# One-token decoder layer on one core: five engine programs with and without a block around them

## Chip, cores and metric

The kernel runs on one core of one Trainium2 chip. Its time is device microseconds of one execution, as the median of three runs. A core has five engines that run programs of their own and meet only through semaphores: TensorE (PE, with its weight loads as PEld), VectorE (DVE), ScalarE (ACT), GpSimd (POOL) and SyncE (SP). SP computes nothing here; it issues nearly all transfers.

## What is computed

Four sequences of one token each go through a pre-norm attention over the last 4096 positions of a key and value cache, and then through a gated network. All tensors are bfloat16.

```python
B, Sq, D = 4, 1, 576;  Hq, Hkv, Sk, Dh = 32, 16, 16384, 128;  F = 4608
W = min(4096, max(256, Sk // 4))
q = (x @ wq).reshape(B, Sq, Hq, Dh).transpose(0, 2, 1, 3)
k = jnp.repeat(k_cache[:, :, Sk - W:, :], rep, axis=1)
v = jnp.repeat(v_cache[:, :, Sk - W:, :], rep, axis=1)
scores = jnp.einsum("bhqd,bhkd->bhqk", q, k) * (Dh ** -0.5)
o = jnp.einsum("bhqk,bhkd->bhqd", softmax(scores), v)
attention = o.transpose(0, 2, 1, 3).reshape(B, Sq, Hq * Dh) @ wo
...
gate = einsum("bsd,df->bsf", x, W_gate);  up = einsum("bsd,df->bsf", x, W_up)
mlp = einsum("bsf,fd->bsd", gate * (gate > 0) * up, W_down)
...
h  = x + attention(layernorm(x))
h2 = h + mlp(layernorm(h))
```

## The kernel before

The window of keys and of values is 67 MB each, and the weights are some 25 MB more, so about 160 MB come in for little arithmetic. The cache is cut into 32 "duos": two key heads of one sequence, 2 MB of keys and 2 MB of values each. Four duos make a batch, so there are 8 batches.

A large tile, `pool`, holds four slots for keys and four for values. The query weights lie in the value slots at first, and the weights of the output projection and of the network take the same room after the attention. `prog_sync` goes through a list of transfers in a fixed order (lines 219 to 256); each waits until the last reader of its place is done. Query weights come first, then keys five duos ahead of the values, then the weights.

`prog_pool` makes constants: it clears tiles (L277 to L279, L283 to L287), builds an identity with an affine select (L280, and a second one at L288), and later finds, for each batch, the largest score over all partitions (L295). `prog_dve` waits for the identity before it builds its selectors (L376) and goes on to the first layer norm; the query projection on PE follows from that. For each half duo of keys DVE transposes the keys (L416), PE multiplies them with the queries (a helper, so nearly all of PE stands at L520), and at the end of a batch DVE takes the maximum (L419), ACT the exponentials (L344), DVE transposes the result (L435) and PE multiplies it with the values. After the last batch come the output projection, the second layer norm, the network's two wide matmuls and the down projection, whose weights come in nine pieces (L256). ACT and DVE write one half of the result each (L363, L513), SP stores it (L270) and waits until the store has landed (`S.wait("sync", "STORED")`).

All five programs are written with a small class, `Sched`. A first pass only counts: it gives every named operation the semaphore value at which it will be done. A second pass emits the instructions, with waits on those values. `S.op` and `S.dma` address the engines through `S.engines`, that is `nc.sync`, `nc.scalar` and so on. In the second pass each program is called by the method of a block for its engine (last lines of the function).

Two places of the code appear in the profile where no operation of the kernel stands. L693 is the line that makes the builder, `_bacc.Bacc(...)`; four constants and a meeting of the five engines come from it. L116 is `with ExitStack() as es:`; what is emitted when the context managers close, the block among them, has this line.

Of the kernel before, what the change touches and what calls it, by code (L numbers as in the profile page):

```python
# [102 lines left out]
def bass_sequential_preLN__sliding_block_cached__glu_gated_reglu__decode_kernel(  # L103
# [12 lines left out]
    with ExitStack() as es:  # L116
# [75 lines left out]
        S = Sched()  # L192
# [479 lines left out]
        progs = [("gpsimd", prog_pool), ("sync", prog_sync), ("scalar", prog_act), ("vector", prog_dve), ("tensor", prog_pe)]  # L672
# [1 line left out]
        for _, p in progs:  # L674
            p(S)
        S.begin(True, nc, es)
        block = es.enter_context(nc.Block())
        for name, p in progs:
            getattr(block, name)(lambda e, p=p: p(S))


# [26 lines left out]
```

## Time and profile before

| | |
|---|---|
| median of 3 runs (lowest to highest) | 383.69 us (383.65 to 383.76) |
| profiled execution: from its first to its last instruction | 382.2 us, 3916 instructions |
| read from memory in it | 159.58 MB, 418 GB/s over the span |
| PE busy | 287.7 us (75%), mean granted clock 0.905 |
| DVE busy | 206.5 us (54%) |
| ACT busy | 53.5 us (14%) |
| POOL busy | 8.2 us (2%) |

The span runs from the first recorded instruction, at 0, to the end of the last one; the records resolve nanoseconds (the last ends at 382.199 us). The time of a run is taken outside the profile and is 1.49 us longer than this span; the trace has no record of those 1.49 us. Waiting is not counted as busy. Engine names with a q (SPq, POOLq) are the engine's sequencer, which runs semaphore, branch, drain and transfer-issuing instructions.

### The profile page before, as it was taken

How to read it: one execution, taken by the hardware profiler on the slowest of the kernel's cores; microseconds unless marked ns; L12 is line 12 of the kernel's file. 1: busy time of each engine (PE TensorE's matmuls, PEld its weight loads, DVE VectorE, ACT ScalarE, POOL GpSimd, SP SyncE). 2: the span in 40 equal slices, each digit the busy share in tenths (PEclk: the TensorE clock that was granted, in tenths of full speed). 3: DMA queues.
4: the chain of work that ended last, by engine and by line, in shares of the span. 5: the costliest groups of instructions: out<-in, count | busy, mean ns of one | idle time of the engine just before them, and what ended most of it. 6: DMA issues, size and time to landing. Idle time of an engine off the chain costs nothing.

```text
span 382.2 us, 3916 instructions
## 1 busy us (share of the span) xinstructions
PE 287.7 (75%) x1697; PEld 124.5 (33%) x1712; DVE 206.5 (54%) x193; ACT 53.5 (14%) x129; POOL 8.2 (2%) x22
## 2 busy tenths in 40 slices
PE   0069749977997799669967996799589796956565
PEld 0053213322432243224322432243224233344331
DVE  0369789369437854774477548744865442042030
ACT  4021050021102110211021103010300021010020
POOL 4100000000000000000000000000000000000000
PEclk9999988997998799989998999899989996965677
DMA  8999999999999999999999999999999999999994
GB/s 307 434 424 422 436 422 429 431 425 427 426 429 430 424 429 430 425 429 429 429 425 430 425 427 432 424 430 427 427 430 425 427 431 424 419 430 424 420 416 198
DMA packets 12417, 159.84 MB, mean 418 GB/s; under 512 B 1384, under 2 KB 1520, under 8 KB 2672
## 3 DMA queue, kind: packets, MB, share of 16 engines
q1 hardware_dynamic: 12392, 159.59, 98.7%
q8 instruction: 13, 0.21, 0.2%
q14 instruction: 4, 0.03, 0.0%
q10 hardware_dynamic: 8, 0.00, 0.0%
HBM read 159.58 MB, written 0.00 MB: 418 GB/s over the span
## 4 chain that ended last, share of the span: by engine, by line
PE 50%; DVE 18%; issue 16%; ACT 6%; DMA 5%; SPq 3%; POOL 1%; POOLq 0%
PE sc L520 27%; PE pb L520 23%; DVE kT L416 6%; ACT P L344 5%; DMA pool<-in_B_W_down_dram 5%; DVE probT L435 4%; DVE rmx L419 4%; SPq L256 3%; POOL bcm L295 1%; DVE P L477 1%; DVE bias L431 0%; DVE rowsum L440 0%; DVE pmax L422 0%; DVE t L427 0%; DVE bmin L429 0%
## 5 line engine op out<-in xcount | busy, mean ns | idle before, releaser
L416 DVE STREAM_TRANSPOSE kT<-pool 128x2048 f32<-128x2048 f32 x64 | 144.5, 2291 | 54.4 <-DMA pool<-in_A_k_cache_dram 47.6
L520 PE MATMUL sc<-kT,qz 128*128 128x512 bf16 x497 | 133.1, 422 | 48.4 <-DVE kT L416 45.1
L520 PE MATMUL pb<-pool,prob 128*16 128x512 bf16 x512 | 118.5, 391 | 0.0
L520 PEld LDWEIGHTS sc<-kT,qz 128*128 128x128 bf16 x512 | 49.2, 102 | 128.6 <-DVE kT L416 53.2
L520 PEld LDWEIGHTS pb<-pool,prob 128*16 128x16 bf16 x512 | 44.0, 92 | 72.4 <-issue 19.0
L344 ACT ACTIVATE P<-sc,bias 128x512 f32<-128x512 f32 x32 | 22.2, 718 | 176.8 <-DVE bias L431 176.8
L419 DVE TENSOR_REDUCE rmx<-sc 128x2 f32<-128x2048 f32 x8 | 18.3, 2292 | 34.9 <-PE sc L520 34.9
L435 DVE STREAM_TRANSPOSE probT<-P 128x2048 f32<-128x2048 f32 x8 | 18.5, 2312 | 7.9 <-ACT P L344 7.9
L527 PE MATMUL pb<-ident_b,xn_bf 4*128 4x4 bf16 (+1 forms) x5 | 0.4, 175 | 19.6 <-ACT xn_bf L308 19.6
L329 ACT COPY cp<-pb 128x512 f32<-128x512 f32 x8 | 4.7, 585 | 67.9 <-PE pb L520 67.9
L520 PE MATMUL pb<-selT,cp 128*128 128x16 f32 x64 | 8.7, 269 | 4.4 <-ACT cp L329 4.4
L520 PEld LDWEIGHTS pb<-selT,cp 128*128 128x128 f32 x64 | 9.0, 208 | 6.5 <-ACT cp L329 5.4
L351 ACT CAST prob<-probT 128x1024 bf16<-128x1024 f32 x8 | 8.4, 1044 | 19.0 <-DVE rs L438 19.0
L444 DVE RECIPROCAL rs_sb<-pb 128x32 f32<-128x32 f32 x4 | 1.4, 339 | 17.8 <-PE pb L520 17.8
L507 DVE TENSOR_TENSOR P<-pb,P 128x288 bf16<-128x288 f32 (+1 forms) x2 | 0.8, 400 | 17.3 <-PE sc L520 17.3
L520 PE MATMUL pb<-pool,probT 128*4 128x288 bf16 x72 | 6.1, 310 | 5.4 <-DMA pool<-in_B_W_down_dram 5.4
L295 POOL PARTITION_ALL_REDUCE bcm<-pmax x8 | 3.1, 388 | 291.5 <-DVE pmax L422 291.5
L322 ACT COPY qz<-qrep 32x64 bf16<-32x64 bf16 x32 | 7.8, 244 | 7.3 <-DVE qrep L453 7.0
L520 PE MATMUL sc<-oX,pool 128*128 128x4 bf16 (+1 forms) x160 | 5.9, 172 | 3.7 <-DVE oX L480 3.7
L520 PE MATMUL pb<-pool,hnT 128*32 128x288 bf16 (+1 forms) x48 | 4.0, 405 | 6.0 <-DMA pool<-in_B_W_up_dram 6.0
L520 PE MATMUL sc<-pool,hnT 128*32 128x288 bf16 (+2 forms) x112 | 6.8, 366 | 0.6 <-DMA pool<-in_B_W_gate_dram 0.6
L520 PEld LDWEIGHTS sc<-oX,pool 128*128 128x128 bf16 (+1 forms) x160 | 5.8, 114 | 4.0 <-issue 3.9
(107 smaller groups left out, 80.1 us busy)
## 6 DMA issues: line engine op xcount, KB each, us to landing
pool<-in_A_k_cache_dram SPq DMA_DIRECT2D x32, 2048.0 KB, 27.9
pool<-in_A_v_cache_dram SPq DMA_DIRECT2D x32, 2048.0 KB, 25.9
pool<-in_A_wo_dram SPq DMA_DIRECT2D x4, 1152.0 KB, 21.7
pool<-in_B_W_gate_dram SPq DMA_DIRECT2D x2, 2304.0 KB, 24.8
pool<-in_B_W_up_dram SPq DMA_DIRECT2D x2, 2304.0 KB, 27.3
pool<-in_A_wq_dram SPq DMA_DIRECT2D x2, 2048.0 KB, 10.1
pool<-in_B_W_down_dram SPq DMA_DIRECT2D x2, 1296.0 KB, 24.1
pool<-in_B_W_down_dram SPq DMA_DIRECT2D x5, 432.0 KB, 25.8
```

The costliest lines, as they stand in the source:

```text
L256: lambda e, g0=g0, g1=g1, j0=j0, nj=nj: e.dma_start(out=wd_sb[:, g0:g1, j0 * D:(j0 + nj) * D], in_=B_W_down[g0 * 128 * JJ:g1 * 128 * JJ, : ...
L295: S.op(g, lambda e, n=n: e.partition_all_reduce(bcm[:, n % 2, :], pmax[:, n % 2, :], 128, bass_isa.ReduceOp.max), deps=deps, name=("PAR", n))
L322: S.op(a, lambda e, src=src, dst=dst: e.copy(out=dst, in_=src), deps=deps, name=("QZ", n) if g == 3 else None, signal=g == 3)
L329: S.op(a, lambda e: e.copy(out=cp[:, n % 2, :], in_=pb[PVB + n % 2]), deps=deps, name=("CP", n))
L344: S.op(a, lambda e, n=n, th=th, u=u: e.activation(out=P[:, th * 1024 + u:(th + 1) * 1024:2], in_=sc[:, th * 1024 + u:(th + 1) * 1024:2], f ...
L351: S.op(a, lambda e, n=n: e.copy(out=prob[:, n % 2, :, :, :], in_=probT[:, :, 0:NHB].rearrange("p t (r x) -> p r t x", x=4)), deps=deps, na ...
L416: S.op(v, lambda e: e.transpose(out=dst, in_=src), deps=deps, name=("TR", i))
L419: S.op(v, lambda e: e.tensor_reduce(out=rmx[:, n % 2, :], in_=sc[:, :].rearrange("p (x u) -> p u x", u=2), axis=AX.X, op=ALU.max), deps=[( ...
L435: S.op(v, lambda e: e.transpose(out=probT[:, :, :].rearrange("p t j -> p (t j)"), in_=P[:, :]), deps=[("EXP", n, 1)] + ([("CMP", n - 1)] i ...
L444: S.op(v, lambda e: e.reciprocal(out=rs_sb[:, b, :], in_=pb[OB][:, 64 + b * H:64 + (b + 1) * H]), deps=[("SUM", b)], name=("RS", b))
L477: S.op(v, lambda e: e.tensor_reduce(out=oS.rearrange("p (x b) -> p x b", b=B), in_=oM.rearrange("p (x s b) -> p x b s", s=8, b=B), axis=AX ...
L520: S.op(t, lambda e: e.matmul(o, lhsT=l, rhs=r, start=start, stop=stop, skip_group_check=skip), deps=deps, name=name, signal=name is not None)
```

## The change

The block is taken away. In the emitting pass the five programs are called one after the other, straight in the function, in the same order as before and as in the counting pass. The programs themselves, their waits, their transfers and the semaphores are the same text; the builder's line moves up by one (L693 becomes L692).

```diff
         S.begin(True, nc, es)
-        block = es.enter_context(nc.Block())
-        for name, p in progs:
-            getattr(block, name)(lambda e, p=p: p(S))
+        for _, p in progs:
+            p(S)
```

## Prediction

> **What bounds the kernel now.** I read the page's transfers and speeds first, then a table by stage, then the records of the two lines that are not the kernel's own work (L693 and L116), and last the start.
>
> ```profile
> DMA  8999999999999999999999999999999999999994
> q1 hardware_dynamic: 12392, 159.59, 98.7%
> ```
>
> The first line is the busy share of the 16 DMA engines in 40 slices, the second SP's and the other hardware queues' packets, MB and share. Only the first and the last slice have room. The table by stage (stretch, its length, then busy time of PE, PEld, DVE, ACT and POOL with counts, granted clock, DMA share, GB/s) says the same in more detail:
>
> ```profile
> 2.00:20.00 18.00, 0.43 (x8) 0.40 (x9) 3.83 (x20) 4.47 (x8) 3.61 (x8) 1.00 0.97 402
> 20.00:100.00 80.00, 63.71 (x372) 26.44 (x377) 60.70 (x47) 13.37 (x36) 0.78 (x2) 0.91 1.01 427
> ...
> 300.00:347.00 47.00, 36.03 (x306) 19.05 (x304) 15.21 (x16) 6.25 (x12) 0.39 (x1) 0.82 1.01 426
> 347.00:370.00 23.00, 12.17 (x223) 7.77 (x223) 3.86 (x18) 2.37 (x6) 0.00 (x0) 0.62 1.00 419
> 370.00:378.00 8.00, 4.44 (x60) 2.12 (x60) 1.93 (x6) 0.00 (x0) 0.00 (x0) 1.00 0.88 355
> 378.00:382.20 4.20, 1.60 (x12) 0.41 (x12) 0.45 (x1) 0.39 (x1) 0.00 (x0) 0.51 0.07 24
> ```
>
> From 2 to some 376 us the transfers set the pace, at 419 to 428 GB/s. What PE, DVE or ACT do earlier or later in between changes nothing, as long as SP's queue does not run dry. Only two places are outside this cover: what lies ahead of SP's first transfer (0 to 0.72 us), and what follows the last weights (378.3 to 382.2 us). The end is this chain (start, length, operation):
>
> ```profile
> 378.33 1.60 PE L520 MATMUL pb<-pool,probT 128*4 128x288 bf16 x12 [0.52 <-DMA pool<-in_B_W_down_dram]
> ...
> 379.98 0.45 DVE L513 CAST out_sb<-pb 4x288 bf16<-4x288 f32 x1 [7.98 <-PE pb L520]
> 380.50 0.35 SPq L270 DMA_DIRECT2D out_dram<-out_sb  x1
> ```
>
> PE ends, ACT and DVE write the halves side by side, SP stores. Behind that only the records of L116 are left (count, duration in ns, first and last start in us):
>
> ```profile
> L116 POOLq EVENT_SEMAPHORE  x2: 17/17/17, 382.0 to 382.1; - x2
> L116 POOLq DRAIN  x1: 502/502/502, 310.3 to 310.3; - x1
> L116 PEldq DRAIN  x1: 585/585/585, 379.4 to 379.4; - x1
> ...
> L116 SPq COMPARE_BRANCH  x1: 32/32/32, 381.8 to 381.8; - x1
> L116 SPq DRAIN  x1: 13/13/13, 382.0 to 382.0; - x1
> L116 SPq EVENT_SEMAPHORE  x1: 17/17/17, 382.1 to 382.1; - x1
> ```
>
> This is the block's end: each engine drains, POOL collects the five signals and releases all. SP comes last, because its branch carries the wait for the store.
>
> **The change part by part.** *The end.* The block's 12 instructions go: five drains, six semaphore instructions, SP's branch. In nanoseconds the records put SP's branch at 381.809, its drain at 381.978, POOL's two semaphore instructions at 382.015 and 382.093, the four releases at 382.136 to 382.148 (PE's lasts 51 ns, to 382.199, the end of the span). Four of the drains lie beside the store or long before it (PE 379.404, ACT 379.985, DVE 379.994, POOL 310.3) and set nothing; SP's path does: 0.032 for the branch, 0.137 from it to the drain, 0.221 from there to the end, 0.390 us together. What stays is the wait for the store. It needs another carrier; SP's semaphore instructions take 17 ns each in these records. Sum of the end: 0.390 − 0.017 = 0.373 us, and the last record ends at 381.809 + 0.017 = 381.826. Bounds of the carrier: 0.017 and the branch's 0.032, so 0.358 to 0.373; I take 0.37.
>
> *The entry.* The block is also entered, and a branch could hide there. SP's release in the builder's meeting (L693) ends at 0.658 and its first transfer issues at 0.721, 63 ns later. POOL's two semaphore instructions at the end stand 61 ns apart (382.032 to 382.093) with nothing in between. So at most 0.002 us is to be had at the entry on SP, and the trace has no branch there. Bounds: 0 and 0.002; I take 0. A loss at the entry isn't excluded and is the slower rival below.
>
> *The five programs.* The instructions, waits and transfers are the same, in the same order on each engine, so 0. Moving the code by a few instructions can move the moment at which instruction pages are fetched (13 packets of the first instruction queue, 4 of the second, 0.2% of the DMA engines' time). All of it lies under the transfers; 0.2% of 382 us is 0.8 us, and a page more would be one packet of 13, or 0.06 us.
>
> *Outside the span.* The runs' median exceeds the span by 383.69 − 382.20 = 1.49 us. No record shows what is in it. If some of it is work at the end that begins when an engine leaves the block, PE, ACT, DVE and POOL could do it earlier: they are done by 379.99, 380.40, 380.48 and 310.8, SP not before 381.83. So between 0 and 1.49 us more could go. The nearest row for what engines do when they leave a meeting is the start: released at 0.60 to 0.65, POOL and ACT issue their first own instruction at 0.717, so nothing but issue follows. I take 0 and keep 1.49 for the range.
>
> The Trainium skill, "Runtime: NRT & Kernel Launch", in "The ~15µs preamble/postamble breakdown", has the runtime add a barrier of its own behind the kernel, about 1.5 us, that waits for all engines, and only then the resets. By it the last engine to arrive still decides, the early ones gain nothing, and the sum remains the 0.37 by which SP arrives sooner; no record of this trace shows that barrier.
>
> **Sum:** the span goes from 382.20 to 381.83; on the median, with the same 1.49 us around it, 383.69 − 0.37 = 383.32 us, 0.10% less. About 0.2% (0.77 us) is what a measurement of this kernel can tell from no change, so this counts as the same.
>
> **The rivals.** *1. The meeting stays (no gain).* The change may not do what it says: something else, the builder's end or the launch, may put an equal meeting behind programs that end without a block. For it: the builder puts one at the start unasked (L693, same drains and semaphores). Against it: the records at the end all have the line of the context managers, none the builder's. Time 383.69.
>
> *2. The end shrinks by more (faster).* Four engines leave 1.3 us or more before SP, and their share of the 1.49 us outside the span goes under SP's wait. For it: 1.49 us is large beside a meeting of 0.37. Against: this time may as well lie ahead of the first record, and SP still has its own share. All of it gives 383.32 − 1.49 = 381.83, half of it 382.57; over 0.40 us of the 1.49 is needed to pass 0.2%.
>
> *3. The start chain gets later (slower).* The chain of waits begins on POOL:
>
> ```profile
> 0.89 3.52 POOL L279 MEMSET qz<- 128x4096 bf16 x1
> 14.82 0.28 POOL L280 TENSOR_SCALAR_AFFINE_SELECT ident_b<-ident_b 128x128 bf16<-128x128 bf16 x1 [10.41 <-issue]
> ```
>
> For 10.4 us POOL does nothing the profile shows between L279 and the affine select; the raw records have two instructions there that change POOL's configuration, and two more at L295. DVE, then ACT, then PE wait for it, until DVE has transposed the first duo and SP may load the fifth one at 28.82. If programs without a block were laid out so that this stall comes twice, or on a cold page, the chain is later by x. The cover: query weights and four duos are queued from the start, 4.5 + 4 × 2 MB (13.11 MB in decimal); by 28.0 us 385 GB/s × 28.0 us = 10.78 MB have landed, the other 2.33 MB last 5.4 us at 429 GB/s, to 33.4. From 28.82, less the 1.04 us from SP's first issue (0.721) to its first packet (1.76), that is 3.5 us. A start later by under 3.5 us costs nothing, beyond it one for one: a second stall of 10.35 us costs 6.8 us, 383.32 + 6.8 = 390.1. For it: the stall is there and nothing in the trace says what sets its length. Against it: POOL's program keeps its order, and the block's entry shows no branch on POOL (release at 0.598 to 0.615, first own instruction at 0.717). That the stall shrinks would bring nothing, since the transfers run full meanwhile (0.97 to 1.01).
>
> **How the numbers follow.** Forecast (0.37 us less) 0.44; rival 1 (no gain) 0.25; rival 2 (faster by more) 0.20; rival 3 (slower) 0.11. So faster 0.20, same 0.44 + 0.25 = 0.69, slower 0.11. The likeliest gives 383.32. For the range I leave out rival 3 whole (0.11) and the third of rival 2 in which over 1 us of the 1.49 goes (0.07): from 383.32 − 1.0 = 382.3 up to rival 1's 383.69 and, for what the moved pages may cost under full queues (at most the 0.5 us that lie between 383.69 and 384.2, two thirds of all that the instruction pages take now), 384.2.
>
> **What would show it.** Right: 3905 instructions (12 fewer, one new carrier of SP's wait), no records on L116 that drain or signal, SP's wait for the store as the last record near 381.83, first transfer still at 0.72, POOL's affine select still near 14.8, GB/s at 419 to 428 in the same stages. Rival 1: drains and semaphores behind the store under another line, span at 382.2. Rival 2: span 381.8 and a median less than 1.1 us above it. Rival 3: the affine select after 18.3 us, and a slice around 33 us with a DMA share clearly below 1.0. The forecast is wrong if the span falls by under 0.2 or over 0.6 us, or if any stretch between 2 and 376 us loses its full transfers.

## The result and the profile after

| | before | after |
|---|---|---|
| median (lowest to highest), 17 runs each | 383.76 us (383.50 to 384.16) | 382.96 us (382.70 to 383.26) |
| ratio, 95% interval | | 0.9977 (0.9970 to 0.9984) |
| span of the profiled execution | 382.2 us | 381.7 us |

The kernel is 0.80 us faster; by the interval, 0.61 to 1.15 us (383.76 × 0.0016 and × 0.0030). The middle of it is just beyond the 0.2% (0.77 us) that the prediction named as the least difference it could tell; the interval reaches to both sides of that.

The page of the kernel after, first the span, then the share of the DMA engines in 40 slices and the main queues:

```profile
span 381.7 us, 3920 instructions
...
DMA  8999999999999999999999999999999999999995
...
q1 hardware_dynamic: 12392, 159.59, 98.8%
```

3920 instructions are recorded, against 3916. The 12 of the block are gone and SP's new wait is there; but 1712 matmuls are recorded against 1697 before. Without these 15, which the trace of before lacks, there would be 3905, the number expected.

The table by stage of the kernel after (busy time of PE, PEld, DVE, ACT and POOL with counts, granted clock, DMA share, GB/s):

```profile
2.00:20.00 18.00, 0.35 (x6) 0.32 (x7) 3.83 (x20) 4.48 (x8) 3.60 (x8) 1.00 0.99 411
20.00:100.00 80.00, 64.22 (x371) 25.95 (x371) 59.82 (x46) 13.36 (x36) 0.78 (x2) 0.85 1.01 426
300.00:347.00 47.00, 36.94 (x305) 19.18 (x303) 15.21 (x16) 6.25 (x12) 0.39 (x1) 0.83 1.01 426
347.00:370.00 23.00, 12.92 (x226) 8.32 (x225) 3.58 (x17) 2.37 (x6) 0.00 (x0) 0.60 1.00 422
370.00:378.00 8.00, 6.07 (x60) 3.16 (x60) 2.21 (x7) 0.00 (x0) 0.00 (x0) 0.64 0.88 354
```

The transfers run as before: no stage differs by more than 9 GB/s. The start and the end, in the timeline of the kernel after (start, length):

```profile
0.72 0.88 SPq L230 DMA_DIRECT2D pool<-in_A_wq_dram  x2
...
14.89 0.28 POOL L280 TENSOR_SCALAR_AFFINE_SELECT ident_b<-ident_b 128x128 bf16<-128x128 bf16 x1 [10.49 <-issue]
...
379.86 0.45 DVE L513 CAST out_sb<-pb 4x288 bf16<-4x288 f32 x1 [7.54 <-PE pb L520]
380.38 0.35 SPq L270 DMA_DIRECT2D out_dram<-out_sb  x1
```

The first transfer goes out at 0.72 as before and the affine select comes at 14.89 instead of 14.82. What follows the store is one record, the second of SP's explicit waits in the last two microseconds (count, ns, first and last start):

```profile
L75 SPq EVENT_SEMAPHORE  x2: 17/17/17, 380.3 to 381.7; - x2
```

It begins at 381.683 and ends the span at 381.700. From the store's issue (380.379) this is 1.32 us; before it was 382.199 − 380.503 = 1.70 us. The difference is 0.38 us, and it is the meeting of the five engines with SP's branch ahead of it. So the span accounts for about half of the 0.80 us.

### The profile page after: what moved, and what is told of

Its sections match the earlier page's. It is cut to its first block, busy times and chain, and to the rows that moved or that the text cites. A ratio compares the mean times of both kernels' runs of the same rounds, so it can differ in the third digit from the quotient of the medians.

```text
span 381.7 us, 3920 instructions
## 1 busy us (share of the span) xinstructions
PE 293.9 (77%) x1712; PEld 125.8 (33%) x1712; DVE 206.8 (54%) x193; ACT 53.4 (14%) x129; POOL 8.2 (2%) x22
## 4 chain that ended last, share of the span: by engine, by line
PE 43%; DMA 23%; DVE 19%; ACT 6%; issue 5%; SPq 3%; POOL 1%; POOLq 0%
PE sc L520 22%; PE pb L520 21%; DMA pool<-in_A_k_cache_dram 18%; DVE kT L416 8%; DMA pool<-in_B_W_down_dram 5%; ACT P L344 4%; DVE probT L435 4%; DVE rmx L419 4%; SPq L256 3%; POOL bcm L295 1%; DVE P L477 1%; DVE bias L431 0%; DVE P L473 0%; DVE rowsum L440 0%; DVE t L427 0%
## 5 line engine op out<-in xcount | busy, mean ns | idle before, releaser
L520 PE MATMUL sc<-kT,qz 128*128 128x512 bf16 x512 | 138.5, 425 | 44.8 <-DVE kT L416 43.0
L520 PE MATMUL pb<-pool,probT 128*4 128x288 bf16 x72 | 7.8, 386 | 3.0 <-DMA pool<-in_B_W_down_dram 2.9
```

What stands on the lines that cost most here:

```text
L520: S.op(t, lambda e: e.matmul(o, lhsT=l, rhs=r, start=start, stop=stop, skip_group_check=skip), deps=deps, name=name, signal=name is not None)
```

## The experiments

One quantity carries them: the **part outside**, the time of a run less the span of the same run, as a mean over the runs. Spans are listed to 0.1 us. The part outside scatters by 0.03 us from run to run, so its mean over 10 runs or more is good to about 0.01 us. The spans scatter by some 0.2 us, and their means are good to 0.05 or 0.1 us only. In the 17 runs of the kernel after it is 1.30 us.

**1. The kernel before once more**, unchanged, to have its spans run by run.

> The kernel before, unchanged, so that its spans are listed run by run. Every theory: ratio to itself 1.000, median 383.7 to 383.8. What it tells apart is the part of a run outside the span (time less span), which is 1.3 us in the changed kernel. Theory A (the whole gain lies inside the span: the meeting's 0.37 us and some 0.4 us that the transfers or the entry gave): outside part 1.3, span 382.4. Theory B (engines that leave early also shorten what lies outside): outside part 1.5, span 382.2 to 382.3.

Measured: median 383.79 us, ratio 0.9998 (0.9990 to 1.0007), mean span 382.02, part outside 1.79; 33 more runs of the kernel before on the same chip give 382.04 and 1.79, and two other chips 1.79 and 1.80. So two things shrink: the span by 0.39 (382.04 to 381.65) and the part outside by 0.49 (1.79 to 1.30). That favours theory B, though its 1.5 was too low.

**2. The meeting alone put back**, without a block.

```diff
         for _, p in progs:
             p(S)
+        nc.all_engine_barrier()
```

> No block, but the builder's meeting of all engines (drains and semaphores) called behind the five programs. If all of the 0.80 us comes from the meeting at the end: back to 383.7, ratio 1.000 to before, span some 0.37 us above the changed kernel's 381.7. If part of it comes from the block's branches and the place of the code: it keeps that part, 0.2 to 0.4 us below before, ratio 0.9990 to 0.9995.

Measured: median 383.70 us, ratio 0.9999 (0.9990 to 1.0007), mean span 381.96, part outside 1.81. The call's records (L679):

```profile
L679 POOLq EVENT_SEMAPHORE  x2: 17/17/17, 381.8 to 381.9; - x2
L679 SPq DRAIN  x1: 7/7/7, 381.8 to 381.8; - x1
L679 SPq EVENT_SEMAPHORE  x1: 17/17/17, 382.0 to 382.0; - x1
...
L679 PEldq EVENT_SEMAPHORE  x1: 51/51/51, 382.0 to 382.0; - x1
```

The same signals as at the block's end, and the whole gain is gone: both the span and the part outside are back. The block's branches and the place of the code gave nothing that the runs can tell; but the interval reaches down to 0.9990, so a gain of up to 0.38 us from them is not excluded by the times alone. In the records SP's way from its wait (381.744) to the end (382.016) is 0.27 us, 0.12 less than with the block's branch; on the time that is below the interval.

**3. No meeting, but all five engines wait for the store.**

```diff
+        for e in ("gpsimd", "scalar", "vector", "tensor"):
+            S.wait(e, "STORED")
```

> No block and no meeting, but POOL, ACT, DVE and PE each wait on the store's semaphore as SP does, so all five leave together. Theory A (only the meeting's own 0.37 us in the span counts): as the changed kernel, ratio 0.9977 to 0.998, outside part 1.3. Theory B (leaving early counts): span as the changed kernel's, outside part back to 1.5, time 383.15 to 383.2, ratio 0.9983 to 0.9985.

Measured: median 383.46 us (383.27 to 384.97), ratio 0.9995 (0.9986 to 1.0003), part outside 1.79. The records of the waits:

```profile
L75 SPq EVENT_SEMAPHORE  x2: 17/17/17, 380.3 to 381.7; - x2
L75 ACTq EVENT_SEMAPHORE  x1: 17/17/17, 381.7 to 381.7; - x1
L75 POOLq EVENT_SEMAPHORE  x1: 17/17/17, 381.7 to 381.7; - x1
L75 DVEq EVENT_SEMAPHORE  x1: 21/21/21, 381.7 to 381.7; - x1
L75 PEldq EVENT_SEMAPHORE  x1: 51/51/51, 381.7 to 381.7; - x1
```

There is no drain and no signal between engines here, and the profiled execution ends at 381.756 against 381.700. Yet the part outside is back at 1.79. So it isn't the meeting that costs those 0.49 us but that the other engines leave late. Theory A falls; theory B is right about the mechanism. The median is still 0.3 us above what theory B gave, because theory B put the part outside at 1.5.

**4. Two meetings**, a second one behind the block of the kernel before.

```diff
-        block = es.enter_context(nc.Block())
-        for name, p in progs:
-            getattr(block, name)(lambda e, p=p: p(S))
+        with nc.Block() as block:
+            for name, p in progs:
+                getattr(block, name)(lambda e, p=p: p(S))
+        nc.all_engine_barrier()
```

> The kernel before with a second meeting of all engines behind the block. The second has no late engine to wait for, so it costs its own chain alone. If the meeting's price is its chain of signals: 0.25 to 0.4 us more than before, 384.0 to 384.15, ratio 1.0007 to 1.001, all of it in the span. If a meeting costs twice that, as the 0.80 us suggest: 384.5, ratio 1.002.

Measured: median 384.10 us (383.88 to 386.69), ratio 1.0013 (1.0000 to 1.0026), part outside 1.77. In the trace the first meeting ends at 381.932, the second at 382.264, 0.33 us later. The median rises by 0.31; the interval begins at 1.0000, for one of the 11 runs is far off (386.69), and the other ten lie between 383.88 and 384.32. So by the trace and the median a meeting with no late engine costs its own chain of signals, all of it in the span; a second one adds nothing outside. The other half of the 0.80 us is paid once, at leaving.

**5 to 8. Which engine is the last.** SP no longer waits for the store; one other engine does. POOL is shown:

```diff
-            S.wait("sync", "STORED")
...
         for _, p in progs:
             p(S)
+        S.wait("gpsimd", "STORED")
```

> No block; the wait for the store stands on POOL instead of SP, so SP leaves at 380.7 us and POOL is the last engine. Theory C (what lies outside the span is work of each engine in a fixed order, and the place of the late engine in that order decides): the part outside differs from the 1.30 us that SP last gave, between 1.1 and 1.8. Theory D (only that the engines don't arrive together matters): 1.30 us whichever engine is last, 382.95 us.

> The same with ACT as the only engine that waits for the store. Theory C: outside part other than 1.30 us by at least 0.05 for some of the four engines. Theory D: 1.30 us, 382.95 us.

> The same with DVE. Theory C: outside part other than 1.30 us, by its place in the order. Theory D: 1.30 us, 382.95 us.

> The same with PE, whose semaphore instruction takes 51 ns instead of 17, so the span is some 0.04 us longer. Theory C: outside part other than 1.30 us, by its place in the order. Theory D: 1.30 us, 382.99 us.

| last engine | median us | ratio (interval) | mean span | part outside |
|---|---|---|---|---|
| SP (the kernel after) | 382.96 | 0.9977 (0.9970 to 0.9984) | 381.65 | 1.30 |
| DVE | 383.05 | 0.9980 (0.9971 to 0.9989) | 381.59 | 1.42 |
| ACT | 382.92 | 0.9982 (0.9973 to 0.9992) | 381.60 | 1.46 |
| PE | 383.37 | 0.9989 (0.9980 to 0.9999) | 381.75 | 1.58 |
| POOL | 383.52 | 0.9996 (0.9987 to 1.0006) | 381.70 | 1.87 |

The waits with POOL last:

```profile
L75 SPq EVENT_SEMAPHORE  x1: 17/17/17, 380.7 to 380.7; - x1
L75 POOLq EVENT_SEMAPHORE  x1: 17/17/17, 382.1 to 382.1; - x1
```

The spans agree within 0.16 us, but the part outside runs from 1.30 to 1.87. Theory D falls. What lies behind the last instruction depends on the engine: with POOL last nearly the whole gain is gone, though there is no meeting and four engines have left. This suggests a simpler form of theory C: each engine has a tail of its own, and the latest end of a tail ends the run. The lengths in the last column serve as tails in the sums below; each also holds whatever of a run lies ahead of its first record, which is the same for all engines. So only their differences are shown, and only these count in the sums.

**9 to 11. Several late engines, and POOL almost late.** These test that form. In 9, POOL waits for the store beside SP; in 10, ACT, DVE and PE do; in 11, POOL waits only until DVE has written its half of the result.

```diff
+        S.wait("gpsimd", "STORED")
```

```diff
+        for e in ("scalar", "vector", "tensor"):
+            S.wait(e, "STORED")
```

```diff
+        S.wait("gpsimd", "OUT1")
```

> No block, SP and POOL both wait for the store, the other three leave early. Theory C' (each engine has a tail of its own behind its last instruction, the latest end counts: 1.87 us for POOL, 1.30 for SP): span 381.65, outside part 1.85 to 1.87, time 383.5. Theory E (the tails add up, or arriving together is what costs): outside part over 2.0, or back at 1.30 if two late engines are not enough.

> No block, SP, ACT, DVE and PE wait for the store, POOL leaves at 310. Theory C' (the latest end counts): the longest tail left is PE's 1.58, so outside part 1.55 to 1.6, span 381.7, time 383.25. Theory E (arriving together costs): outside part 1.75 or more, as with all five.

> No block, SP waits for the store, and POOL waits until DVE has written its half of the result, so POOL leaves 1.3 us before SP instead of 71 us. Theory C': POOL's end is 1.3 us earlier than SP's last instruction plus 1.87, so 0.57 after it, under SP's own 1.30: outside part 1.30, time 382.95. Theory F (POOL has to be away long before, since its tail is longer than the row suggests or holds up others): outside part above 1.35.

Measured: with POOL beside SP, part outside 1.85, median 383.52 us, ratio 0.9992 (0.9983 to 1.0002). With the three others, 1.56, median 383.44 us, 0.9989 (0.9980 to 0.9999); that is 0.2 us above the time expected, all of it in the spans (mean 381.88). With POOL leaving at the cast, 1.30, median 382.87 us, 0.9975 (0.9966 to 0.9985). The waits of the last one:

```profile
L75 SPq EVENT_SEMAPHORE  x2: 17/17/17, 380.2 to 381.5; - x2
L75 POOLq EVENT_SEMAPHORE  x1: 17/17/17, 380.2 to 380.2; - x1
```

POOL leaves at 380.23 and its tail ends at 380.23 + 1.87 = 382.10; SP leaves at 381.57 and its tail ends at 381.57 + 1.30 = 382.87, against 382.89 measured for this execution. So a POOL that leaves 1.3 us before SP costs nothing. By these tails 1.87 − 1.30 = 0.57 us before SP would be enough, which no run tests. Theories E and F fall. The same sum gives the kernels with a meeting. In the first profile of before POOL sends the release at 382.093 and leaves 0.017 later; 382.110 + 1.87 − 382.199 = 1.78 outside the span, measured 1.79. In experiment 2 it is 381.928 + 1.87 − 382.016 = 1.78, measured 1.81. In experiment 3 POOL's wait ends at 381.717, so 381.717 + 1.87 − 381.756 = 1.83, measured 1.79; the sums are good to 0.04 us.

One rival is left. Theory C as it was first put, one round through the engines in a fixed order, gives the same sums: if POOL came first in the round and SP last, an engine's tail would be what remains of the round behind it, and again the latest end would count. No run here tells such a round from tails of the engines' own.

**12. A later start**, for the price of the third rival: POOL clears `qz` three times.

```diff
-            S.op(g, lambda e: e.memset(qz[:, :, :, :, :].rearrange("p a r c m -> p (a r c m)"), 0.0), name="QZ0")
+            S.op(g, lambda e: e.memset(qz[:, :, :, :, :].rearrange("p a r c m -> p (a r c m)"), 0.0), name="QZa")
+            S.op(g, lambda e: e.memset(qz[:, :, :, :, :].rearrange("p a r c m -> p (a r c m)"), 0.0), deps=["QZa"], name="QZb")
+            S.op(g, lambda e: e.memset(qz[:, :, :, :, :].rearrange("p a r c m -> p (a r c m)"), 0.0), deps=["QZb"], name="QZ0")
```

> No block, and POOL clears qz three times instead of once, so that the start chain is 7.0 to 7.1 us later (affine select at 21.9). By the working of the cover (3.5 us are free, beyond it one for one): 3.5 us more than the changed kernel, 386.5, with the transfers running dry near 33 us. If the transfers have more cover than worked out, less, down to no change at 382.95; if nothing is covered, 390.

Measured: median 388.21 us of 4 runs (387.50 to 389.33), ratio 1.0109 (1.0092 to 1.0126), 5.3 us more than the kernel after and 1.7 us more than expected. The affine select of this run:

```profile
22.17 0.28 POOL L282 TENSOR_SCALAR_AFFINE_SELECT ident_b<-ident_b 128x128 bf16<-128x128 bf16 x1 [10.63 <-issue]
```

The table by stage, first of this run:

```profile
20.00:33.00 13.00, 5.36 (x159) 4.96 (x159) 6.49 (x24) 0.87 (x1) 1.20 (x7) 1.00 1.00 426
33.00:39.00 6.00, 3.76 (x12) 1.53 (x13) 5.82 (x5) 3.25 (x9) 0.00 (x0) 1.00 0.32 90
39.00:46.00 7.00, 7.00 (x33) 2.97 (x31) 7.00 (x4) 0.00 (x0) 0.00 (x0) 1.00 0.95 389
46.00:100.00 54.00, 40.32 (x147) 14.36 (x148) 39.60 (x30) 8.67 (x22) 0.78 (x2) 0.81 1.01 428
```

Then of the kernel after:

```profile
33.00:39.00 6.00, 6.00 (x28) 2.58 (x27) 6.00 (x4) 0.00 (x0) 0.00 (x0) 1.00 1.02 434
39.00:46.00 7.00, 5.06 (x22) 1.66 (x19) 4.93 (x3) 0.00 (x0) 0.00 (x0) 1.00 0.99 424
```

The transfers run dry at the place that the working gave, but the cover was smaller. The select is 22.17 − 14.89 = 7.28 us later. From 33 to 46 us this run moves 6 × 90 + 7 × 389 = 3263 KB, the kernel after 6 × 434 + 7 × 424 = 5572 KB. The 2309 KB between them are 5.4 us at 428 GB/s, and that is the whole of the 5.3 us. If the start counts one for one beyond the cover, the cover was 7.28 − 5.3 = 2.0 us, not 3.5; a single length of delay can't show whether it does. The working also reckoned with a quick and complete restart. In the records SP issues the fifth duo at 36.17 and its first packet starts at 37.51, 1.34 us later instead of 1.04, and from 39 to 46 us the transfers are still 35 GB/s short. The profiled execution is the slowest of the four (span 388.0 us); what it lost beyond this lies at its end and isn't followed up.

## Why the prediction was right and where it was not

**What bounds the kernel: right.** The stages run at the same speeds. From 370 to 378 us PE had a clock of 0.64 instead of 1.00, and the transfers moved 354 GB/s instead of 355.

**The end, 0.373 us: right.** The store's issue to the end of the span went from 1.70 to 1.32 us, 0.38; the mean spans differ by 0.39.

**The entry and the programs, 0: right.** The compiled programs of before hold one unconditional branch at the block's entry on each engine, which the trace doesn't record. From SP's release to its first transfer it was 63 ns with it and is 64 ns without.

**Outside the span, taken as 0: this is the term that was mis-sized.** It measured 0.49 us, more than the end itself. Two things were wrong in that step. The 1.49 us were a median less the span of a single execution; run by run the part is 1.79 us. With that the profiled execution of before took, by estimate, 382.20 + 1.79 = 383.99 us, above all three runs of the first table; no record gives its own time. And the value came from the release at the start, where an engine only goes on to its next instruction. Nothing there says what an engine does when its program is over. The bounds that were written down, 0 to 1.49, hold the 0.49; the sum took the lower one.

The Trainium skill, "Runtime: NRT & Kernel Launch", in "The ~15µs preamble/postamble breakdown", lists a barrier for all engines behind the kernel. The step drew from it that early engines gain nothing. Here they do: SP waits for the store in each of these runs, and the part outside is 1.30, 1.56, 1.79 or 1.85 us, depending on which others wait beside it. A barrier may still be in it. But work behind a barrier for all engines would begin at the same time whichever came last; so what differs between the engines lies ahead of such a barrier, or in the order in which it takes them.

**The rivals.** The first (the meeting stays) did not come about, and experiment 2 shows that it would have left the time as before. The second was the case: "over 0.40 us of the 1.49 is needed to pass 0.2%", and 0.49 went. Its sign, a median less than 1.1 us above the span, did not come: it is 1.26 us above it, since this limit was reckoned from 1.49 and not from 1.79. It named the four early engines; of these POOL is the one that mattered: by the sums above its tail is the longest, and the meeting kept it to the end. The third did not happen; experiment 12 bears out its place but not its price, with some 2 us of cover for 3.5.

**The sum:** 0.37 forecast; 0.38 at the end and 0.49 outside are 0.87, against 0.80 (0.61 to 1.15) measured between the medians. The time lies in the range, 0.36 us below the forecast. It does so because the range left room for the part outside, not because the sum had it: the sum holds less than half of the gain. The median falls a little beyond the 0.2% line, on the side that was given 0.20, and the interval covers both sides.

## What to carry to other kernels

A meeting of all engines at the end of a kernel costs twice: its own chain of signals, and the time by which it holds back engines that could begin to end. Leave the last wait to the engine with the smallest part outside (SP here; by the times alone DVE and ACT can't be told from it), and let the others go as soon as their own work is done. When a time is larger than a span, take both from the same run, and ask for each engine what follows its last instruction.

## What the runs showed of the hardware

The time of a run exceeds its span by 1.30 us when SP is the last engine, by 1.42 with DVE, 1.46 with ACT, 1.58 with PE and 1.87 with POOL. With several late engines the latest end, reckoned with these figures, counts. How much of the 1.30 us lies ahead of the first record is not shown. What an engine does behind its last instruction no record shows either, so why POOL takes longest stays open, and whether it is work of its own or its place in an order. None of the other versions is clearly better than the kernel after: 382.87 and 382.92 us against 382.96 lie within their intervals.
